# Order of the attention steps, the pool of the transposes and the first products of a fused attention and mixture kernel

## The chip, the core and the metric

The kernel runs on one core of a Trainium2 chip. Time is the device time of one execution in microseconds (us). TensorE multiplies, VectorE and ScalarE take results out of PSUM and work on SBUF, GpSimd works on SBUF alone, and SP issues nearly all transfers.

## What is computed

Three layers, one behind the other. Inputs are drawn at random.

```python
def _attn_ref(q, k, v):                       # 4 batches, 8 heads, 576 positions, 64 features
    scores = scale * np.matmul(q, k.transpose(0, 1, 3, 2))
    mask_local = (rel >= 0) & (rel < stride)  # stride = 32, heads 0 to 3
    mask_strided = (rel >= 0) & (pos[None, :] % stride == pos[:, None] % stride)   # heads 4 to 7
    ...                                       # softmax over the masked scores
    return np.matmul(attn, v)

def _moe_ref(x, w_gate, w1, w2):              # 2304 tokens of 512, 8 experts of 1024
    ...                                       # P: 8 rounds of row and column normalization of the gate
    for e in range(E):
        out += P[:, e:e + 1] * (np.maximum(x @ w1[e], 0.0) @ w2[e])

def _moe2_ref(x, w_in, w_out):                # 512 to 2048 to 512
    h = x @ w_in
    return np.where(h > 0.0, h, np.exp(np.minimum(h, 0.0)) - 1.0) @ w_out
```

## The kernel before, in words

Attention is done in 32 steps `u`, two for each of 16 pairs of heads; two local steps (u % 4 is 0 or 1) alternate with two strided ones (2 or 3). A step has three stages. `att_s2(u)` makes scores: a mask product with the full array (line 529), then products of q and k of 64 features in quarters of the array (line 543). VectorE takes the maximum and subtracts it (552, 553), ScalarE exponentiates (556), VectorE sums (559) and takes reciprocals (564), GpSimd multiplies by them (567, "normalization"). `att_s3` transposes the result on TensorE (605 for local steps, full array; 590 for strided ones, half of the columns), ScalarE copies it out. `att_s4` multiplies by v (628 local, half of the columns; 644 strided, quarters). In step u these run for u, u - 2 and u - 3. What follows the scores is not issued at once: `defer` puts it off by a number of ticks, one tick at each yield of the attention generator, by the tables `DEF_FIRST`, `DEF_ALONE` and `DEF_MIXED`.

The program is written out by Python generators, and the order in which they are advanced is the order of each engine's instructions; no scheduler changes it. Up to step 20 ("mix") attention runs alone, with some products of the mixture put in between: from step 12 on, one "group" of six products of 512 columns behind each step. From step 20 on a piece of attention (four advances of its generator) runs every few `gap`s between products. A gap comes about every three products and also advances the weights' splitting (`prep_step`), the splitting of x (`build_step`) and the gate.

All products of the mixture are made in three matmuls of a high and a low part (xh, xl, w1h, w1l). The first two pairs of 128 features of expert 0 use the features as they are ("direct", lines 1080 to 1105); later ones use sums of quarters (`gemm1`, `gemm2` is the second layer, line 1247). The sums are built from `build_sums` on VectorE (line 379), cast to xh on ScalarE (385) and to xl on VectorE and GpSimd (217). Before the second layer of the first pair all builds that are left are issued at once (`ready("sums")`).

PSUM has two pools of four banks: `bank()` (ps) for scores and first-layer products, `ybank()` (py) for the second layer. `spare_bank()` gives a bank of the first pool while the second layer runs and one of the second otherwise. `warm_up` puts a matmul without use (line 452) into a new bank to keep TensorE busy, until the first "group".

## Time and profile before

| | |
|---|---|
| median of 3 runs | 1992.93 us (1991.99 to 1992.95) |
| the profiled execution | 1992.91 us, of which the span of the core 1991.0 us |
| TensorE busy in the span | 1972.8 us (99%), 10563 matmuls |
| VectorE, ScalarE, GpSimd busy | 1240.1 us, 683.7 us, 601.0 us |
| attention | about the first 165 us |

A busy TensorE is not one at its peak: matmuls overlap, so what counts is the distance from start to start, and idle time where it waits. A row of the timeline gives start, length, engine, line of the kernel, what is written and read, how many instructions are merged, and in brackets how long the engine was idle before and what ended it.

### The profile page before, as it was taken

Reading aid. Unit: us, or ns where it says so; the run is one execution under the profiler, and the core shown is the slowest. Engines: PE = TensorE matmul, PEld = TensorE weight load, DVE = VectorE, ACT = ScalarE, POOL = GpSimd, SP = SyncE. Lnnn points to the kernel's source line nnn. Section 1 sums busy time; section 2 is a strip of 40 time slices with the busy share of each in tenths; the row PEclk is TensorE's granted clock in tenths of the full one; section 3 lists DMA queues with packets and bytes.
Section 4 is the critical chain, followed back from the end, with each engine's and each line's share of the span. In section 5 each row is a group of like instructions: output and inputs, shape, how many; then the busy total and the mean of one; then the engine's idle time right before and its main releaser. Section 6 shows DMA issues by size and latency. Waiting matters only on the chain.

```text
span 1991.0 us, 27182 instructions
## 1 busy us (share of the span) xinstructions
PE 1972.8 (99%) x10563; PEld 1633.1 (82%) x10563; DVE 1240.1 (62%) x2078; ACT 683.7 (34%) x1414; POOL 601.0 (30%) x690
## 2 busy tenths in 40 slices
PE   9999999999999999999999999999999999999999
PEld 7777888888888888888888888888888888887887
DVE  6657666555455657566666666666664485568665
ACT  5543332233223334222222222222222264446543
POOL 4533332333333332222232222222222212233340
PEclk9999999999999999999999999999999999999999
DMA  7422211111113112122222222222221111212111
GB/s 219 146 84 66 64 50 47 53 53 54 53 42 106 54 53 85 64 75 90 75 69 85 80 85 71 83 80 85 65 69 43 43 32 33 85 43 96 43 54 53
DMA packets 82786, 140.79 MB, mean 71 GB/s; under 512 B 5760, under 2 KB 39808, under 8 KB 82656
## 3 DMA queue, kind: packets, MB, share of 16 engines
q1 hardware_dynamic: 81696, 138.83, 22.2%
q8 instruction: 83, 1.36, 0.3%
q14 instruction: 47, 0.39, 0.1%
q10 hardware_dynamic: 960, 0.21, 0.1%
HBM read 121.20 MB, written 17.83 MB: 70 GB/s over the span
## 4 chain that ended last, share of the span: by engine, by line
PE 91%; DVE 4%; ACT 3%; issue 1%; DMA 0%; POOL 0%; DVEq 0%; ACTq 0%; POOLq 0%
PE ybank L1247 48%; PE bank L1017 40%; ACT g L1040 1%; ACT g L1039 1%; DVE u L1131 1%; PE bank L543 1%; ACT hh L1044 1%; DVE xl L217 0%; DVE c L1131 0%; PE ybank L628 0%; PE ybank L605 0%; DVE hl L1034 0%; PE ybank L590 0%; ACT w1h L207 0%; DMA k_t<-in_k 0%
## 5 line engine op out<-in xcount | busy, mean ns | idle before, releaser
L1247 PE MATMUL ybank<-w2h,hh 128*128 128x512 f32 x1280 | 501.8, 392 | 0.3
L1247 PE MATMUL ybank<-w2h,hl 128*128 128x512 f32 x1280 | 499.0, 390 | 0.0
L1247 PE MATMUL ybank<-w2l,hh 128*128 128x512 f32 x1280 | 498.7, 390 | 0.0
L1017 PE MATMUL bank<-xh,w1h 128*128 128x512 f32 x1124 | 443.0, 394 | 3.8 <-DVE u L1131 3.7
L1017 PE MATMUL bank<-xl,w1h 128*128 128x512 f32 x1124 | 438.1, 390 | 0.0
L1017 PE MATMUL bank<-xh,w1l 128*128 128x512 f32 x1124 | 437.9, 390 | 0.0
L217 POOL TENSOR_TENSOR w1l<-w1raw,w1h 128x256 fp32r<-128x256 f32 x244 | 211.1, 886 | 425.4 <-ACT w1h L207 425.2
L1278 DVE SCALAR_TENSOR_TENSOR acc<-ybank,prob,acc 128x512 f32<-128x512 f32 x244 | 182.8, 749 | 229.1 <-PE ybank L1247 228.5
L217 POOL TENSOR_TENSOR w2l<-w2raw,w2h 128x512 fp32r<-128x512 f32 x80 | 103.9, 1298 | 600.0 <-ACT w2h L207 579.5
L1247 PEld LDWEIGHTS ybank<-w2h,hh 128*128 128x128 f32 x1280 | 240.8, 188 | 51.8 <-DVE acc L1264 1.6
L1247 PEld LDWEIGHTS ybank<-w2h,hl 128*128 128x128 f32 x1280 | 240.6, 188 | 50.6
L1247 PEld LDWEIGHTS ybank<-w2l,hh 128*128 128x128 f32 x1280 | 240.8, 188 | 49.0
L207 ACT CAST w2h<-w2raw 128x512 fp32r<-128x512 f32 x160 | 97.1, 620 | 463.4 <-issue 406.7
L1017 PEld LDWEIGHTS bank<-xh,w1h 128*128 128x128 f32 x1124 | 211.1, 188 | 53.3 <-DVE u L1131 8.0
L1017 PEld LDWEIGHTS bank<-xh,w1l 128*128 128x128 f32 x1124 | 211.0, 188 | 44.9
L1017 PEld LDWEIGHTS bank<-xl,w1h 128*128 128x128 f32 x1124 | 211.3, 188 | 40.3
L1131 DVE TENSOR_TENSOR u<-bank,a 128x512 f32<-128x512 f32 x152 | 105.0, 691 | 195.2 <-PE bank L1017 163.4
L236 POOL TENSOR_TENSOR wsum<-w1raw 128x256 f32<-128x256 f32 x152 | 117.5, 773 | 227.7 <-DMA w1raw<-in_moe_w 159.4
L1032 ACT ACTIVATE hh<-bank 128x512 fp32r<-128x512 f32 x193 | 114.8, 595 | 117.6 <-DVE bank L1131 110.7
L1034 DVE SCALAR_TENSOR_TENSOR hl<-bank,hh 128x512 fp32r<-128x512 f32 x193 | 131.8, 683 | 7.1 <-ACT hh L1032 0.9
L217 DVE TENSOR_TENSOR w1l<-wsum,w1h 128x512 fp32r<-128x512 f32 x152 | 112.4, 747 | 10.0 <-ACT w1h L207 8.9
L1032 ACT ACTIVATE hh<-c 128x512 fp32r<-128x512 f32 x61 | 38.6, 633 | 224.4 <-DVE c L1131 224.4
(229 smaller groups left out, 2401.5 us busy)
## 6 DMA issues: line engine op xcount, KB each, us to landing
w1raw<-in_moe_w SPq DMA_DIRECT2D x64, 512.0 KB
w2raw<-in_moe_w SPq DMA_DIRECT2D x64, 512.0 KB
raw<-in_moe_w_in SPq DMA_DIRECT2D x16, 512.0 KB
w_conv<-val SPq DMA_DIRECT2D x32, 256.0 KB
raw<-in_moe_w_out SPq DMA_DIRECT2D x16, 512.0 KB
w1raw<-w_conv SPq DMA_DIRECT2D x16, 512.0 KB
w2raw<-w_conv SPq DMA_DIRECT2D x16, 512.0 KB
q_t<-in_q SPq DMA_DIRECT2D x16, 288.0 KB
```

The lines of the kernel that those rows point to most:

```text
L207: se.copy(hi, src)
L217: eng.tensor_tensor(out=lo, in0=src, in1=hi.bitcast(F32), op=ALU.subtract)
L236: po_.tensor_tensor(out=o, in0=x, in1=y, op=op)
L543: pe.matmul(pp[part][r : r + w, i * nk : (i + 1) * nk], t["q"][dd, qc : qc + w], t["k"][dd, kc : kc + nk], start=False, stop=i == len(mine ...
L1017: pe.matmul(dst, a_[:, wi, c, :], b_[:, xi, c, :], start=start and i == 0, stop=stop and i == 5, skip_group_check=True,)
L1032: se.activation(hh, src, AF.Relu)
L1034: ve.scalar_tensor_tensor(out=hl, in0=src, scalar=0.0, in1=hh.bitcast(F32), op0=ALU.max, op1=ALU.subtract)
L1039: se.activation(g, src, AF.Relu, scale=-1.0)
L1040: se.activation(g, g, AF.Exp, scale=-1.0)
L1131: ve.tensor_tensor(out=out, in0=x, in1=y, op=ALU.add)
L1247: pe.matmul(y, x[:, cs], w[:, f], start=first and f + m == 0, stop=last and f == 1 and m == 2)
L1278: ve.scalar_tensor_tensor(out=at, in0=y, scalar=prob[:, g, e : e + 1], in1=at, op0=ALU.mult, op1=ALU.add)
```

## The change

In the attention part: in steps above 3 with u % 4 of 2 or 3 the transposition comes first, then scores, then values; in the other steps scores, values, transposition. This holds alone and mixed (mixed had values, transposition, scores). The transposition always takes a bank of the second pool. The first products come in a new generator, `first_parts`: each part does one chunk of 128 features for both quarters, and leaves its bank open until the other chunk's part. Ten of the 16 parts run in steps 9, 10 and 12 to 19 (before: eight, in steps 12 to 19). After the second layer starts, attention waits for `HOLD` = 4 gaps. q and k of the second pair are loaded ahead of v of the first. Five constants differ.

```diff
-            pt = warm_up(ybank() if alone_now[0] else spare_bank())
+            pt = warm_up(ybank())
...
-            for gen in (s2, s4, s3, s3) if alone_now[0] else (s4, s3, s3, s2):
+            for gen in (s3, s3, s2, s4) if u > 3 and u % 4 > 1 else (s2, s4, s3, s3):
...
-            if MOE_FROM <= u < MIX_FROM:
+            if u in GROUP_AT:
                 yield "group"
...
+    load_qk(1)
     load_v(0)
-    load_qk(1)
...
+            while second[0] and count[0] < second[1] + HOLD:
+                yield True
...
+    def first_parts():
+        order = [(0, 0, f, c) for c in (0, 1) for f in (0, 1)] + [(1, 0, f, c) for f in (0, 1) for c in (0, 1)]
+        order += [(0, 1, f, c) for c in (0, 1) for f in (0, 1)] + [(1, 1, f, c) for f in (0, 1) for c in (0, 1)]
+        open_ = {}
+        for p, half, f, c in order:
+            prep_state["now"] = p
+            w = slot_of(p, "done1")
+            m = open_.setdefault((p, half, f), None) if c else open_.setdefault((p, half, f), bank())
+            keys = ("B12", B22) if half else (B11, B21)
+            for i, (wi, key) in enumerate(zip((S1, A22) if f else (A11, A12), keys)):
+                need(key, c)
+                for a_, b_ in ((0, 0), (0, 1), (1, 0)):
+                    pe.matmul(m, w[a_][:, wi, c, :], xb[b_][:, T1 if key == "B12" else key, c, :], ...)
...
-        second[0] = True
+        second[:] = [True, count[0]]
...
-WARM0, WARM1, WARM_MOD, WARM_OF, WARM_N = 14, 10, 4, 1, 512
+WARM0, WARM1, WARM_MOD, WARM_OF, WARM_N = 12, 10, 4, 1, 512
-W1_AT, W2_AT = 3, 9
+W1_AT, W2_AT = 2, 9
-DEF_ALONE, DEF_MIXED = (2, 4, 5, 6), (2, 3, 4, 5)
-PREP_AT = 24
-MOE_FROM, MIX_FROM, ATT_RATE = 12, 20, 0.8
+DEF_ALONE = DEF_MIXED = 2, 4, 5, 6
+PREP_AT = 20
+MIX_FROM, ATT_RATE = 20, 0.8
+GROUP_AT = (9, 10, 12, 13, 14, 15, 16, 17, 18, 19)
+HOLD = 4
```

What stands on the engines, at three places. First TensorE in step 18 (attention alone), before, from the last product of step 17's group to the first of step 18's: masks and scores (529, 543), values (644), transposition (605).

```order
L1017 MATMUL bank<-xh,w1l_84 128x512
L529 LDWEIGHTS eye
L529 MATMUL bank<-m_str,eye 118x162
L529 LDWEIGHTS eye
L529 MATMUL bank<-m_str,eye 118x162
L543 MATMUL bank<-k_t,q_t 54x54 x12
L644 MATMUL ybank<-eT,v_t 64x54 x10
L605 MATMUL ybank<-ident,e_local_113 96x128 x5
L1017 MATMUL bank<-xh,w1h_83 128x512
```

The same stretch after.

```order
L1094 MATMUL bank<-xh,w1l_84 128x512
L605 MATMUL ybank<-ident,e_local_113 96x128 x5
L529 LDWEIGHTS eye
L529 MATMUL bank<-m_str,eye 118x162
L529 LDWEIGHTS eye
L529 MATMUL bank<-m_str,eye 118x162
L543 MATMUL bank<-k_t,q_t 54x54 x12
L644 MATMUL ybank<-eT,v_t 64x54 x10
L1094 MATMUL bank<-xh,w1h_81 128x512
```

The transposition moved from the end of the step to its head, right behind the group of the step before. Second, TensorE in step 23 (mixed), before: values (628), transposition, masks and scores, then the second layer.

```order
L628 MATMUL bank<-eT,v_t 64x64 x10
L605 MATMUL bank<-ident,e_local_114 96x128 x4
L529 LDWEIGHTS eye
L529 MATMUL bank<-m_str,eye 118x162
L529 LDWEIGHTS eye
L529 MATMUL bank<-m_str,eye 118x108
L543 MATMUL bank<-k_t,q_t 54x54 x10
```

And after.

```order
L605 MATMUL ybank<-ident,e_local_114 96x128 x4
L529 LDWEIGHTS eye
L529 MATMUL bank<-m_str,eye 118x162
L529 LDWEIGHTS eye
L529 MATMUL bank<-m_str,eye 118x108
L543 MATMUL bank<-k_t,q_t 54x54 x10
L628 MATMUL bank<-eT,v_t 64x64 x10
```

The values moved behind the scores, and the transposition writes to the second pool. Third, VectorE around the reciprocal of step 20 (`rc`, sums `sm` of e_local_113), before.

```order
L553 TENSOR_TENSOR e_local_114<-ybank,ng 128x2x96
L564 RECIPROCAL rc<-sm 128x5
L379 TENSOR_TENSOR acc<-acc 128x512
L1034 SCALAR_TENSOR_TENSOR hl<-bank,hh 128x512
L217 TENSOR_TENSOR w1l_82<-wsum,w1h_81 128x512
L559 TENSOR_REDUCE sm<-e_local_114 128x4
L217 TENSOR_TENSOR xl<-acc,xh 128x512 x2
```

And after.

```order
L553 TENSOR_TENSOR e_local_114<-ybank,ng 128x2x96
L559 TENSOR_REDUCE sm<-e_local_113 128x5
L379 TENSOR_TENSOR acc<-acc 128x512
L217 TENSOR_TENSOR xl<-acc,xh 128x512 x2
L1036 SCALAR_TENSOR_TENSOR hl<-bank,hh 128x512
L217 TENSOR_TENSOR w1l_82<-wsum,w1h_81 128x512
L564 RECIPROCAL rc<-sm 128x5
```

Step 20's reciprocal now stands behind the last builds of the sums; its sum, too, is behind step 21's subtraction.

## Rows read from the trace of the kernel before

**Rows 1.** The page: shares of the chain that ended last; one group's mean.

```profile
PE 91%; DVE 4%; ACT 3%; issue 1%; DMA 0%; POOL 0%; DVEq 0%; ACTq 0%; POOLq 0%
...
L1034 DVE SCALAR_TENSOR_TENSOR hl<-bank,hh 128x512 fp32r<-128x512 f32 x193 | 131.8, 683 | 7.1 <-ACT hh L1032 0.9
```

**Rows 2.** Stretches: length; PE, PEld, DVE, ACT, POOL busy (count); clock; DMA.

```profile
80.00:90.00 10.00, 8.23 (x101) 5.69 (x98) 9.93 (x19) 6.26 (x15) 5.77 (x4) 0.99 0.51 156
90.00:100.00 10.00, 9.80 (x81) 7.26 (x79) 4.30 (x14) 5.76 (x13) 4.17 (x4) 0.84 0.29 84
...
400.00:500.00 100.00, 100.00 (x443) 82.67 (x442) 55.73 (x84) 33.51 (x68) 34.04 (x42) 1.00 0.17 53
```

**Rows 3.** Timeline of TensorE at the start: start, length, instruction [idle before, releaser].

```profile
10.40 0.52 PE L543 MATMUL bank<-k_t,q_t 64*54 64x54 f32 x24 [1.18 <-DMA k_t<-in_k]
...
13.31 0.84 PE L605 MATMUL ybank<-ident,e_local 128*96 128x128 f32 x3
```

**Rows 4.** Timeline of GpSimd at the start: the first normalization.

```profile
11.18 0.99 POOL L567 TENSOR_TENSOR e_local<-e_local,rc 128x480 f32<-128x480 f32 x1 [1.01 <-DVE rc L564]
```

**Rows 5.** Transfers in the first 45 us.

```profile
DMA packets 5983, 10.34 MB, mean 230 GB/s; under 512 B 1192, under 2 KB 2600, under 8 KB 5976
```

**Rows 6.** Timeline of TensorE, attention alone: steps 6, 10, 14 and 18.

```profile
23.01 0.30 PE L529 MATMUL bank<-m_str,eye 118*118 118x162 bf16 x2
...
24.87 0.75 PE L605 MATMUL ybank<-ident,e_local 128*96 128x128 f32 x5 [0.75 <-POOL e_local L567]
...
33.90 0.50 PE L452 MATMUL ybank<-warm 128*128 128x512 f32 x1
...
46.03 0.30 PE L529 MATMUL bank<-m_str,eye 118*118 118x162 bf16 x2
...
47.29 0.75 PE L605 MATMUL ybank<-ident,e_local 128*96 128x128 f32 x5 [0.17 <-POOL e_local L567]
...
59.65 0.30 PE L529 MATMUL bank<-m_str,eye 118*118 118x162 bf16 x2
```

**Rows 7.** Timeline of GpSimd: normalizations for the transpositions of steps 14 and 18.

```profile
45.98 1.26 POOL L567 TENSOR_TENSOR e_local<-e_local,rc 128x480 f32<-128x480 f32 x1 [2.73 <-DVE rc L564]
...
59.60 0.99 POOL L567 TENSOR_TENSOR e_local<-e_local,rc 128x480 f32<-128x480 f32 x1 [1.71 <-DVE rc L564]
```

**Rows 8.** Timeline of TensorE: scores before values (step 13) and before products (step 21).

```profile
42.95 0.56 PE L543 MATMUL bank<-k_t,q_t 64*64 64x96 f32 x16
43.33 0.52 PE L644 MATMUL ybank<-eT,v_t 54*64 54x54 f32 x24
...
80.39 0.56 PE L543 MATMUL ybank<-k_t,q_t 64*64 64x96 f32 x16
80.88 0.50 PE L1017 MATMUL bank<-xh,w1h 128*128 128x512 f32 x1
```

**Rows 9.** Timeline of TensorE in the mixed part: steps 20, 22 and 27.

```profile
73.04 0.69 PE L628 MATMUL ybank<-eT,v_t 96*64 96x64 f32 x16
...
74.27 0.38 PE L529 MATMUL ybank<-m_local,eye 128*128 128x96 bf16 x3
...
85.31 0.56 PE L644 MATMUL bank<-eT,v_t 54*64 54x54 f32 x20
...
87.52 0.42 PE L605 MATMUL bank<-ident,e_local 128*96 128x128 f32 x2 [1.20 <-ACT xlate L654]
88.52 0.30 PE L529 MATMUL bank<-m_str,eye 118*118 118x162 bf16 x2 [0.58 <-DVE hl L1034]
...
121.53 0.21 PE L529 MATMUL ybank<-m_str,eye 118*118 118x108 bf16 x1 [1.06 <-ACT xlate L636]
```

**Rows 10.** Timeline of VectorE: step 20's reciprocal and xl casts.

```profile
82.90 0.18 DVE L564 RECIPROCAL rc<-sm 128x5 f32<-128x5 f32 x1
...
85.43 2.43 DVE L217 TENSOR_TENSOR xl<-acc,xh 128x512 fp32r<-128x512 f32 x2
...
98.03 0.65 DVE L217 TENSOR_TENSOR xl<-acc,xh 128x512 fp32r<-128x512 f32 x1
```

More of the change, by code (lines that the diff above doesn't have):

```diff
@@ L602, in att_s3 @@
             n = min(3, len(tiles) - i0)
-            pt = warm_up(ybank() if alone_now[0] else spare_bank())
+            pt = warm_up(ybank())
             for i in range(n):
@@ L871, in sparse_attention_moe_kernel @@
     gens = []
-    second, hurry = [False], [0]
+    second, hurry = [False, 0], [0]
     def spare_bank():
@@ L1077, in gemm1_two @@
         return hs
+    def first_parts():
[10 more added lines that the diff above has]
+                for a_, b_ in ((0, 0), (0, 1), (1, 0)):
+                    pe.matmul(
+                        m,
+                        w[a_][:, wi, c, :],
+                        xb[b_][:, T1 if key == "B12" else key, c, :],
+                        start=c + i + a_ + b_ == 0,
+                        stop=c + i == 2 and a_ == 1,
+                        skip_group_check=True,
+                    )
+                if i == 0 and not alone_now[0]:
+                    gap()
+            used(p)
+            if c:
+                acts.append(activate(p, m, HALF, h_first[p][f, half]))
+            advance(acts)
+            if not alone_now[0]:
+                gap()
+            yield
     def direct_parts(sg, p):
@@ L1416, in sparse_attention_moe_kernel @@
     rest = None
-    first = [direct_parts(0, p) for p in range(GROUP)]
-    h_first = [next(x) for x in first]
-    parts = (next(x) for x in first for _ in range(4))
+    h_first = [{(f, half): new_h(p) for half in (0, 1) for f in (0, 1)} for p in range(GROUP)]
+    first = first_parts()
     for x in att_gen:
@@ L1424, in sparse_attention_moe_kernel @@
             warming[0] = False
-            next(parts, None)
+            next(first)
             continue
@@ L1475, in memory @@
         return x
-    for x in first:
-        for _ in x:
-            pass
+    for _ in first:
+        pass
     start_build("T1", build_both(T1, b_raw, (ve, po_)))
```

## The prediction, made before the changed kernel was timed

> **What bounds the kernel now.** I read the chain of work first, then the table by stretches, then TensorE's timeline of the attention part beside those of VectorE, GpSimd and the transfers. The chain is TensorE for 91% [rows 1], and in a late stretch TensorE is busy for all of 100 us with 443 matmuls, one start each 0.226 us [rows 2]. The change leaves the number of product matmuls as it is, and nothing after attention is rewritten, so only the first 165 us can move: what counts is TensorE's waste there. It has four kinds: idle while it waits (1.18 us for k_t at 10.40, 0.75 at 24.87, 0.17 at 47.29, 1.20 at 87.52, 1.06 at 121.53) [rows 3, 6, 9]; warm-up matmuls whose result nobody reads [rows 6]; the gap when the array goes from one tile shape to another [rows 8]; and a stretch at half clock: 0.84 granted in 90 to 100 us, that is the 1.2 GHz level for a third of it [rows 2], right after the worst stall. The profiled execution took 1992.91 us with a span of 1991.0; its 1.9 us outside don't change. It is the median of the runs to 0.02 us, so the sum is made against it.
>
> **The start: -1.4 us.** q and k of the second pair are issued ahead of v of the first. v is 96 x 1216 words, 467 KB; at the mean of 230 GB/s [rows 5] k_t lands some 2 us earlier and the 1.18 us are gone [rows 3]. WARM0 takes two matmuls off the head: 0.45 us by the pitch above. The step that then counts is the first transposition of e_local: it started at 13.31 [rows 3], although its operand was ready at 11.18 + 0.99 = 12.17 [rows 4]. With the head 0.45 earlier the operand is there at 11.7; TensorE, 1.18 earlier at 12.1 if the five fillers run as now. So 12.1 less the 13.31 is -1.2, up to -1.6 if they run faster; I take -1.4. The lower bound is -0.4, if k_t gains nothing. v of the first pair now lands later but is first read after these transpositions, 2 us or more away; without that cover it would cost what k_t gains. The first weights' load (W1_AT) is ahead of one pair's q and k on SP's queue: 512 KB, 2.2 us at that rate, while those are read several steps later; I cost it at nothing, 2.2 us if the cover fails.
>
> **Warm-up: -1.3 us.** The warm-ups stop at the first "group", now at step 9. Three of 17 go. One is 0.50 long [rows 6], of which the next group overlaps a little; between 0.23 (the pitch) and 0.50 I take 0.43, so 3 x 0.43. Two products more lie ahead of the mix and two fewer behind it: moved, not saved.
>
> **The new order while attention is alone: +3.5 us.** In steps 6, 7, 10, 11, 14, 15, 18, 19 the transpositions go ahead of scores and values. Scores and values gave the softmax of two steps before time to end; in every fourth step (6, 14, 18; step 10 has the new product at step 9 ahead of it) that cover is gone. The number of tile shape changes doesn't fall here, since a full-array product or mask stands before and after either way. Step 6: TensorE got to its masks at 23.01; the operand was used at 24.87 [rows 6], after an idle 0.75. Started first, it waits 1.86, so +1.1. Step 14: TensorE was free at 46.03, GpSimd's normalization ended at 45.98 + 1.26 = 47.24 [rows 6, 7]: 1.21 + 0.05 less the 0.17 now, +1.1. Step 18: free at 59.65, ready at 59.60 + 0.99 = 60.59 [rows 6, 7]: +0.95. Together +3.1. Behind each wait stand scores and values in TensorE's queue, and VectorE waits for the scores, so nothing fills it. Four smaller places have no row: step 12's scores need a bank of the first pool, of which two are now held open from step 9 to 13; product 14 needs weights that GpSimd makes behind a normalization; steps 8 and 9 transpose strided heads later. Bounds 0 and 1.5; I take 0.4, near the 0.17 that such waits cost now.
>
> **The order in the mixed part: -2.0 us.** Scores followed by values in the same 64x64 shape take 43.33 - 42.95 = 0.38; the same scores followed by a full product take 80.88 - 80.39 = 0.49 [rows 8]: a change of shape costs 0.11 us. Four successive steps have 17 changes now (4, 5, 4, 4) and 11 after (3, 3, 2, 3). Three such rounds have scores: 3 x 6 x 0.11 = 2.0. Bounds 1.3 (two thirds of them seen) and 2.5.
>
> **Transposes in the second pool, HOLD: -0.2 us in sum.** Scores no longer queue behind a copy for a bank: the 1.06 at 121.53 [rows 9] should fall to about 0.4, since the values, now last, still want a bank that ScalarE frees: -0.7, bounds -1.1 and +0.4. New waits of transpositions that go first in steps 22 to 31 have no row; one such wait costs 0.17 to 1.86 in the alone part, but here 15 matmuls (3.4 us) lie between scores and transposition. Bounds 0 and 2.5, I take 0.5.
>
> **Step 20, the costliest place: 0.** In before the burst began at 85.31 and TensorE stood idle for 1.20 and 0.58 in it [rows 9]: 1.8 of waste. The cause is the builds of the sums, all issued at once before the second part's products. After, the reciprocal of step 20 stands behind them: one more subtraction, two xl casts, one hl and one w1l are ahead of it. The casts took 2.43 [rows 10], the other three about 0.68 each by hl's mean [rows 1]: 4.5. Its scores start 74.27 - 73.04 = 1.2 us earlier, as values and transposition no longer stand ahead of them [rows 9], so the reciprocal goes from 82.90 [rows 10] to 82.9 + 4.5 - 1.2 = 86.2, and with a normalization as long as the 1.26 of step 14 [rows 7] the operand is there at 87.4. TensorE comes at 85.0 (85.31 less three changes of shape in the two bursts before): 2.4 of waste instead of 1.8. If the casts run at the 0.65 of a lone one [rows 10], it is 1.3 (1.13 less). I take no change, bounds -1.0 and +1.5. HOLD's delay doesn't shorten this: 30 matmuls lie between the scores and the transposition before and after. The half-clock stretch behind it I leave: 0, bound -1.7 (a third of 10 us at half speed).
>
> **The sum.** -1.4 - 1.3 + 3.1 + 0.4 - 2.0 - 0.7 + 0.5 + 0 = -1.4: 1992.9 - 1.4 = **1991.5 us**. A measurement of this kernel can tell some 0.2%, 4 us: below 1988.9 is faster, above 1996.9 slower.
>
> **Rivals.**
> (a) The stall at step 20 closes and the clock stays up: -1.8 there instead of 0, -1.7 for the clock. With 1991.5 that gives 1988.0, faster. For it: the low clock follows the stall, and ScalarE, which also made TensorE wait there [rows 9], is freed by the later transposition. Against: VectorE is busy 9.93 of 10 us in 80 to 90 [rows 2], and the reciprocal goes to the end of that queue. Chance 0.26.
> (b) The transposition at the head waits in the mixed part too. In the alone part the operand comes 1.2 us after TensorE is free for it (47.24 against 46.03), behind what VectorE has to do for the next step's scores; in the mixed part VectorE also has the combinations of products in that queue. It decides once that queue takes longer than the 15 matmuls (3.4 us) and the values that lie between. Steps 22, 23, 26, 27, 30, 31 at 1.0 to 1.2 each (the price of step 14) instead of 0.5 in sum: +6.2, so 1997.7, slower. Against: among TensorE's waits after 75 us none is for a normalization, though there too VectorE had both. Chance 0.14.
> (c) The order saves no drain, because a shape change hides under weight loads or waits that come anyway: the -2.0 is not there, 1993.5, within 0.2%. Against: the two intervals of 0.38 and 0.49. Chance 0.15.
> (d) The waits of the alone part don't come, since VectorE reaches the sums earlier there: -3.1, 1988.4, just faster. Chance 0.06; the ends of the normalizations in rows 7 speak against it.
> (e) The two moved casts bring their whole contended length into the path of step 20: 2.4 instead of 1.8, +0.6, so 1992.1, within 0.2%. Two took 2.43 while GpSimd made the same casts for the other half; a lone one took 0.65 [rows 10]. Chance 0.05. The Trainium skill, "SBUF — State Buffer", section "SBUF: two separate sides", says that GpSimd and a VectorE instruction with two SBUF inputs take turns on a port pair, each locking it for a whole instruction; the trace agrees in that the casts are longer in that company, and by that rule this is the case that comes.
>
> **How the numbers follow.** The forecast as worked out has 0.34. Its own bounds run from 1989.9 (start -1.6, step 20 -0.5, none of the smaller and the mixed waits) to 1996.2 (start -0.4, smaller waits 1.5, mixed waits 2.5, step 20 +0.6), so it lies within 0.2%. Same: 0.34 + 0.15 + 0.05 = 0.54. Faster: 0.26 + 0.06 = 0.32. Slower: 0.14. The range goes 1 us below rival (a) and stops short of (b), 1986.9 to 1996.9: below it lies a small part of (a), above it most of (b), less than 0.2 together.
>
> **What would show it.** After the change: no idle for k_t, the first transposition of e_local near 12; three fewer warm-ups; idle ended by GpSimd before transpositions at steps 6, 14, 18, of 1 to 2 us each, which are my largest cost; bursts of the mixed part shorter by 0.1 to 0.3 us each; one idle piece at step 20 of 1 to 3 us, ended by GpSimd where ScalarE ended it, and a stretch at half clock after it. I am wrong if those waits of the alone part are missing, if the clock is 1.00 from 80 to 110 us, or if anything after attention differs by more than 1 us.

## The result and the profile after

The changed kernel takes 2002.65 us (2002.28 to 2003.48), against 1992.46 us for the kernel before in the same comparison: 1.0052 times as long, interval 1.0040 to 1.0065. That is 11 us above the forecast and 6 us above its range. With every term at its worst bound (covered loads left out) the prediction's sum would have ended near 1999.5, so the miss is not one of sizes alone.

The span of the profiled execution is 2001.7 us, against 1991.0. To see where the 10.7 us lie I cut both traces at two instructions that both programs have: the second block of gate products (L661, 67.36 us in before, 76.95 after), which comes right after the mix begins, and the first product behind attention (L916, now L918; 169.91 and 188.58). Columns: stretch; its length; busy time of PE, PEld, DVE, ACT, POOL (count); granted clock; DMA. The first stretch begins with the first mask of step 0. Before:

```profile
6.25:67.36 61.11, 58.65 (x1035) 45.32 (x1034) 42.79 (x129) 37.81 (x96) 30.36 (x45) 0.97 0.78 229
67.36:169.91 102.55, 98.10 (x1063) 72.97 (x1063) 62.99 (x150) 45.64 (x107) 38.95 (x44) 0.98 0.27 86
```

After:

```profile
6.44:76.95 70.51, 61.84 (x1044) 47.05 (x1043) 43.18 (x128) 37.16 (x95) 31.20 (x46) 0.98 0.66 194
76.95:188.58 111.63, 103.97 (x1093) 79.99 (x1093) 67.97 (x155) 48.54 (x112) 37.91 (x44) 0.97 0.26 79
```

Alone, the part is 9.4 longer; 12 products that were moved into it take 2.7 (0.226 each), which leaves **+6.7**. TensorE is not busy for 8.7 us there, against 2.5. Mixed, the part is 9.1 longer; 30 more matmuls (1093 against 1063) are 6.8 of that, which leaves **+2.3**. The rest of the program has 42 products fewer (9.5 us) and is only 8.0 shorter: **+1.5**, in code that the change doesn't touch. Busy times of VectorE, ScalarE and GpSimd in the first part hardly differ: no engine has more to do, TensorE waits more often. These are the waits (timeline of TensorE, attention alone; steps 6, 8, 12, 14, 16 and 18), which answer to [rows 6]:

```profile
23.39 0.75 PE L605 MATMUL ybank<-ident,e_local 128*96 128x128 f32 x5 [1.67 <-POOL e_local L567]
30.36 0.83 PE L590 MATMUL ybank<-ident,e_str 118*64 118x118 f32 x12 [1.22 <-POOL e_str L567]
...
41.99 0.30 PE L529 MATMUL bank<-m_local,eye 128*128 128x96 bf16 x2 [1.50 <-DVE e_str L553]
42.47 0.24 PE L529 MATMUL bank<-m_local,eye 128*128 128x192 bf16 x1 [0.18 <-DVE e_str L553]
...
53.64 0.75 PE L605 MATMUL ybank<-ident,e_local 128*96 128x128 f32 x5 [1.56 <-POOL e_local L567]
62.42 0.83 PE L590 MATMUL ybank<-ident,e_str 118*64 118x118 f32 x12 [0.47 <-POOL e_str L567]
...
69.03 0.75 PE L605 MATMUL ybank<-ident,e_local 128*96 128x128 f32 x5 [0.84 <-POOL e_local L567]
```

And in the mixed part (steps 21, 22, 25, 29 and 31; what step 22 transposes is step 20's), which answer to [rows 9]:

```profile
90.07 0.83 PE L590 MATMUL ybank<-ident,e_str 118*64 118x118 f32 x12 [0.61 <-ACT xlate L654]
...
97.86 1.30 PE L605 MATMUL ybank<-ident,e_local 128*96 128x128 f32 x5 [2.53 <-POOL e_local L567]
...
119.64 0.83 PE L590 MATMUL ybank<-ident,e_str 118*64 118x118 f32 x12 [0.66 <-DVE e_local L553]
...
147.80 0.82 PE L590 MATMUL ybank<-ident,e_str 118*64 118x118 f32 x12 [0.66 <-DVE e_local L553]
...
161.07 0.80 PE L628 MATMUL ybank<-eT,v_t 96*64 96x64 f32 x20 [1.68 <-issue]
```

After three of the longest waits, and after one of 1.85 us at 1844, TensorE ran at the 1.2 GHz level for a while (table of stretches of the changed kernel; the last column but two is the granted clock):

```profile
40.00:50.00 10.00, 8.32 (x155) 6.50 (x151) 5.43 (x16) 5.15 (x13) 2.62 (x3) 0.83 0.45 133
...
100.00:110.00 10.00, 10.00 (x105) 8.32 (x101) 4.24 (x13) 5.74 (x14) 5.66 (x7) 0.94 0.44 136
160.00:170.00 10.00, 8.93 (x58) 6.54 (x60) 7.40 (x18) 2.59 (x7) 1.02 (x1) 0.83 0.17 54
1840.00:1850.00 10.00, 8.15 (x30) 6.21 (x29) 7.62 (x11) 6.76 (x13) 5.46 (x5) 0.83 0.17 54
```

The kernel before had two such stretches, near 11 and 90 us. What one costs can be read off directly: two executions of the same program up to 66 us, one with such a stretch in the alone part (the row 6.25:67.36 above, clock 0.97) and one without (the kernel called before_phase_other below):

```profile
6.17:65.64 59.47, 57.24 (x1035) 44.17 (x1035) 42.77 (x129) 37.75 (x96) 30.33 (x45) 1.00 0.77 233
65.64:166.58 100.94, 96.49 (x1063) 71.80 (x1063) 63.01 (x150) 45.57 (x107) 38.87 (x44) 1.00 0.28 88
```

61.11 - 59.47 = **1.64 us** for one stretch; the mixed parts of the two, with the same idle time, give 1.61. In what follows lengths are compared at full clock, with 1.64 taken off for each such stretch (some later traces have a stretch of twice the length; the clock column then shows 0.95 over the alone part instead of 0.97 or 0.98): 59.5 for the alone part of the kernel before, 100.9 for its mixed part. The medians of many executions hold the average of the stretches that come and go.

### The profile page after: what moved, and what is told of

Read it like the earlier page. It is cut to its first block, busy times and chain, and to the rows that moved or that the text cites. A ratio compares the mean times of both kernels' runs of the same rounds, so it can differ in the third digit from the quotient of the medians.

```text
span 2001.7 us, 27163 instructions
## 1 busy us (share of the span) xinstructions
PE 1974.5 (99%) x10558; PEld 1635.1 (82%) x10558; DVE 1241.8 (62%) x2078; ACT 683.7 (34%) x1414; POOL 597.9 (30%) x690
## 4 chain that ended last, share of the span: by engine, by line
PE 92%; DVE 4%; ACT 3%; issue 1%; POOL 1%; POOLq 0%; ACTq 0%; DVEq 0%
PE ybank L1280 48%; PE bank L1019 39%; PE bank L1094 1%; ACT g L1042 1%; ACT g L1041 1%; DVE u L1164 1%; PE ybank L590 1%; ACT hh L1046 0%; PE bank L543 0%; PE ybank L605 0%; DVE xl L217 0%; POOL e_local L567 0%; DVE c L1164 0%; DVE g L1044 0%; PE ybank L628 0%
## 5 line engine op out<-in xcount | busy, mean ns | idle before, releaser
L1019 PE MATMUL bank<-xh,w1h 128*128 128x512 f32 x1092 | 430.7, 394 | 4.1 <-DVE u L1164 3.9
L1019 PE MATMUL bank<-xl,w1h 128*128 128x512 f32 x1092 | 426.8, 391 | 0.0
L1019 PE MATMUL bank<-xh,w1l 128*128 128x512 f32 x1092 | 426.4, 391 | 0.0
L1019 PEld LDWEIGHTS bank<-xh,w1h 128*128 128x128 f32 x1092 | 205.6, 188 | 53.3 <-DVE u L1164 7.9
L1019 PEld LDWEIGHTS bank<-xh,w1l 128*128 128x128 f32 x1092 | 205.6, 188 | 43.9
L1019 PEld LDWEIGHTS bank<-xl,w1h 128*128 128x128 f32 x1092 | 205.8, 189 | 39.7
```

The costliest lines, as they stand in the source:

```text
L1019: pe.matmul(dst, a_[:, wi, c, :], b_[:, xi, c, :], start=start and i == 0, stop=stop and i == 5, skip_group_check=True,)
```

## The experiments

In each, "before" is the time of the kernel before on the same chip in the same comparison.

**The counter at the hand-over.** The plus 1.5 far from the change needs a cause. The generator that mixes the work counts gaps, and in the second half of the mixture builds of sums are skipped at every third count. Since two first products moved ahead of the mix, where no gap is counted for them, the count is 4 lower from there to the end, and 4 is not a multiple of 3. Two kernels shift that line alone.

```diff
-        if not part2 or count[0] % 3:
+        if not part2 or (count[0] + 1) % 3:
```

> The changed kernel, with the counter of gaps advanced by one in the single line that skips every third build of sums in the second half of the mixture: (count + 1) % 3. Nothing before the last quarter of the program reads this line. Theory P (phase): two of the first products moved ahead of the mix, the counter is 4 lower from there on, 4 is not a multiple of 3, so builds and casts at the hand-over to the third layer come in another order; there TensorE waits 0.56 and 1.85 us (before: 1.64 alone) and a stretch at half clock follows. Advanced by one, the order is that of the kernel before: some 3 us come back, 1999.7, no half clock after 1800 us. Rival D (drift): the hand-over is late because everything is some 8 us later against the transfers; then nothing comes back, 2002.6.

```diff
-        if not part2 or count[0] % 3:
+        if not part2 or (count[0] + 2) % 3:
```

> The kernel before, with (count + 2) % 3 in the same line, which is the phase that the changed kernel has there. Theory P: it loses what the changed kernel loses at the hand-over: 1992.5 + 2.9 = 1995.4, with waits of about 0.6 and 1.8 us near 1830 and a half-clock stretch behind them. Rival D: 1992.5.

after_phase: 2001.30 us (1999.39 to 2002.16), where the changed kernel had 2002.65 and, on another chip, 2003.78. before_phase: 1993.70 (before 1992.84; ratio 1.0004, interval 0.9994 to 1.0014). The medians alone wouldn't decide, the rows do. Timeline of TensorE at the hand-over from the second to the third layer, in the changed kernel:

```profile
1834.83 0.47 PE L1019 MATMUL bank<-xh,w1h 128*128 128x512 f32 x1 [0.56 <-DVE u L1164]
1844.14 0.50 PE L1019 MATMUL bank<-xh,w1h 128*128 128x512 f32 x1 [1.85 <-DVE u L1164]
```

after_phase has one wait there:

```profile
1841.63 0.50 PE L1019 MATMUL bank<-xh,w1h 128*128 128x512 f32 x1 [1.64 <-DVE u L1164]
```

In the kernel before:

```profile
1835.07 0.50 PE L1017 MATMUL bank<-xh,w1h 128*128 128x512 f32 x1 [1.64 <-DVE u L1131]
```

And in before_phase:

```profile
1826.20 0.47 PE L1017 MATMUL bank<-xh,w1h 128*128 128x512 f32 x1 [0.56 <-DVE u L1131]
1835.51 0.50 PE L1017 MATMUL bank<-xh,w1h 128*128 128x512 f32 x1 [1.87 <-DVE u L1131]
```

The pattern goes with the phase, in both kernels and both ways: theory P holds, drift falls. Counted from the end of the program, matmuls 700 to 500 take 47.3 us in before and after_phase, 48.7 in before_phase, and 50.3 in the changed kernel, where the clock fell behind the second wait. So the phase costs 1.5 us, and 3.0 in executions where the clock falls; it fell in three of the seven traces with this pattern. In before_phase's trace it didn't, and its median lies 1.7 below the 1995.4 of theory P.

The third phase:

```diff
-        if not part2 or count[0] % 3:
+        if not part2 or (count[0] + 1) % 3:
```

> The kernel before with (count + 1) % 3 in the line that skips every third build late in the program: the phase that neither kernel has. Theory P: the wait at the hand-over to the third layer depends on this phase; in the other two it is 1.64, or 0.56 and 1.87. This one lies at 0.8 to 2.5 us in sum, 1991.5 to 1993.2, and nothing before 1600 us changes. Rival D: 1.64, as before.

1992.18 us (before 1992.29; 0.9999, 0.9990 to 1.0008), with the single wait of 1.64 again. Of three phases one loses, and the change fell on that one. This trace has no stretch at half clock before its last microsecond (span 1988.1 us), and so it is the measure for the others.

**The order while attention is alone.**

```diff
-            for gen in (s3, s3, s2, s4) if u > 3 and u % 4 > 1 else (s2, s4, s3, s3):
+            for gen in (s3, s3, s2, s4) if u > 3 and u % 4 > 1 and not alone_now[0] else (s2, s4, s3, s3):
```

> The changed kernel with the order of before (scores, values, transposition) in the steps in which attention is alone; mixed steps keep the new order. Theory H (head): the waits for GpSimd at the head of steps 6, 8, 10, 14, 16, 18 (1.67, 1.22, 0.19, 1.56, 0.47, 0.84) fall to those of before (0.75, 0.18, 0.17): -4.9, 1997.8. If the wait of 1.68 at step 12 and the half clock behind it also come from that order, -8, 1994.6. Rival M (moved): VectorE is the bound of this part, the waits come back at other places, 2001 to 2003.

1997.65 us (before 1992.84; ratio 1.0022, 1.0012 to 1.0031), 5.0 below the changed kernel's first median, as theory H has it. The head waits went, and the step-12 wait with them. Two others appeared, in the products:

```profile
48.76 0.75 PE L605 MATMUL ybank<-ident,e_local 128*96 128x128 f32 x5 [0.63 <-POOL e_local L567]
52.05 0.79 PE L1094 MATMUL bank<-xh,w1l 128*128 128x512 f32 x1 [1.97 <-POOL w1l L217]
74.29 0.50 PE L1094 MATMUL bank<-xl,w1h 128*128 128x512 f32 x1 [0.74 <-POOL xl L217]
```

The first products now reach weights, and once a part of x, before GpSimd has split them; the new order had hidden this by being late itself. Idle in the alone part fell by 3.1 (8.7 to 5.6), so rival M, by which all of it only moves, falls, though 2.7 us did move to these two places. The ten runs lie apart: three took 1993.0 to 1994.3 us at a mean granted clock of 0.999 to 1.000, seven 1997.0 to 1999.6 at 0.996 to 0.997, so the 5.0 between the medians hold the clock too. The same question from the other side, the new order in the kernel before, in the alone steps and nowhere else:

```diff
-            for gen in (s2, s4, s3, s3) if alone_now[0] else (s4, s3, s3, s2):
+            for gen in ((s3, s3, s2, s4) if u > 3 and u % 4 > 1 else (s2, s4, s3, s3)) if alone_now[0] else (s4, s3, s3, s2):
```

> The kernel before with the new order (transposition, scores, values) in steps 6, 7, 10, 11, 14, 15, 18, 19 alone; all else as before, and no bank is held open. Theory H: the order alone brings the head waits of the changed kernel, 1.67, 1.22, 1.56, 0.47, 0.84 at steps 6, 8, 14, 16, 18 in place of 0.75, 0.18, 0.17: +4.7, and it makes the subtraction of step 11 so late that step 12 waits 1 us or more though no bank is held: +5.7, 1998.2. Theory B (banks held open are half of it): no wait at step 12, the wait at step 8 not there either since the heads behind it differ: +3.1 as the prediction had it, 1995.5.

1999.42 us (before 1992.29; ratio 1.0043, 1.0027 to 1.0060; four runs of 1997.8 to 2004.0): **+7.1 us** from this line alone. Its stretches, alone and mixed:

```profile
6.88:73.88 67.00, 59.36 (x1035) 45.29 (x1034) 43.00 (x128) 37.29 (x95) 30.75 (x46) 0.97 0.70 204
73.88:174.84 100.96, 96.51 (x1064) 71.81 (x1063) 63.25 (x150) 45.90 (x108) 37.81 (x43) 1.00 0.27 88
```

The mixed part is that of before to 0.02 us; the alone part is 67.0 - 1.64 - 59.5 = 5.9 longer at full clock, and 5.4 of that is idle (7.6 against 2.2). The waits up to step 14:

```profile
23.82 0.75 PE L605 MATMUL ybank<-ident,e_local 128*96 128x128 f32 x5 [1.68 <-POOL e_local L567]
29.82 0.83 PE L590 MATMUL ybank<-ident,e_str 118*64 118x118 f32 x12 [0.24 <-POOL e_str L567]
34.93 0.75 PE L605 MATMUL ybank<-ident,e_local 128*96 128x128 f32 x5 [1.76 <-POOL e_local L567]
42.87 0.83 PE L590 MATMUL ybank<-ident,e_str 118*64 118x118 f32 x12 [0.44 <-POOL e_str L567]
50.75 0.75 PE L605 MATMUL ybank<-ident,e_local 128*96 128x128 f32 x5 [1.10 <-POOL e_local L567]
```

Steps 16 and 18 wait 0.47 and 0.84, as in the changed kernel. Step 10 waits 1.76 here, where no product stands at step 9; with that product, in the changed kernel, it waits 0.19. Step 12's scores don't wait here, where no bank is held, and step 8 waits 0.24 instead of 1.22. In size theory H is right, in its account of steps 8 and 12 theory B. So I took the held bank away in the changed kernel.

```diff
-        order = [(0, 0, f, c) for c in (0, 1) for f in (0, 1)] + ...
+        order = [(0, 0, f, c) for f in (0, 1) for c in (0, 1)] + ...
```

> The changed kernel with the first four parts in the order quarter by quarter instead of chunk by chunk, so that one bank of the first pool is held open and only from one part to the next (steps 9 to 10), none at step 12. Theory B (banks): the 1.50 and 0.18 at step 12 are scores without a bank; they go, and the stretch at half clock behind them with them: -1.7 - 1.7, 1999.3. Rival L (late): the subtraction of step 11 is late because of the waits at the heads; the wait stays whatever is held, 2002.6. The weights of the second chunk are needed one part earlier, which may cost up to 1 us at step 10.

2001.90 us (before 1992.84; 1.0046, 1.0031 to 1.0061): nothing gained that can be told from the changed kernel's 1.0052. The wait at step 12 is gone, so the bank was what the scores waited for; but TensorE's busy time in the alone part (62.02 of 70.72) says that just as much is lost elsewhere:

```profile
40.37 0.50 PE L1094 MATMUL bank<-xh,w1h 128*128 128x512 f32 x1 [1.11 <-ACT xh L207]
...
46.62 0.83 PE L590 MATMUL ybank<-ident,e_str 118*64 118x118 f32 x12 [0.80 <-POOL e_str L567]
```

Banks explain where the wait stood, not that there is one: neither theory as put.

**The first products.** What they cost when everything else is put back (old orders, old pool and mixed table, `HOLD` 0, phase of before):

```diff
-            for gen in (s3, s3, s2, s4) if u > 3 and u % 4 > 1 else (s2, s4, s3, s3):
+            for gen in (s2, s4, s3, s3) if alone_now[0] else (s4, s3, s3, s2):
...
-            pt = warm_up(ybank())
+            pt = warm_up(ybank() if alone_now[0] else spare_bank())
...
-        if not part2 or count[0] % 3:
+        if not part2 or (count[0] + 1) % 3:
...
-DEF_ALONE = DEF_MIXED = 2, 4, 5, 6
+DEF_ALONE, DEF_MIXED = (2, 4, 5, 6), (2, 3, 4, 5)
-HOLD = 4
+HOLD = 0
```

> The changed kernel with everything put back but the first products and the start: old order alone and mixed, transposes in the pool of before, HOLD = 0, old table for the mixed part, the phase of the counter as before. What is left: products by chunk from step 9 on in ten parts, the load order, 12 warm-ups at the head and the two start counts of the splitting. Theory W (weights): three warm-ups fewer give -1.3, but products come before GpSimd has split their weights: waits of about 2.0 at step 15 and 0.7 at step 19, seen with the old order alone; +1.4, and step 20 as before: 1993.7. Rival: those waits come from the mixed table or the pool; then -1.3, 1991.0.

1995.81 us (before 1992.29; 1.0018, 1.0008 to 1.0028): +3.5, with the waits of 1.97 and 0.75 as expected. That is 2.1 more than theory W had. Its trace has stretches at half clock (0.95 over the alone part, 0.97 over the mixed one), a wait of 1.49 at 128.95 where before has 1.06, and one for step 20's operand, though the mixed order is the old one:

```profile
95.00 1.20 PE L605 MATMUL bank<-ident,e_local 128*96 128x128 f32 x5 [2.17 <-POOL e_local L567]
```

Here the reciprocal had ended at 90.64; the normalization stood behind a cast of xl on GpSimd itself (91.94 to 93.54). Now the same with eight parts from step 12 on, without the shift of the phase:

```diff
-GROUP_AT = (9, 10, 12, 13, 14, 15, 16, 17, 18, 19)
+GROUP_AT = (12, 13, 14, 15, 16, 17, 18, 19)
```

> As the kernel with only the new first products left (old orders, old pool, old mixed table, HOLD = 0), but they begin at step 12 in eight parts; with eight parts ahead of the mix the counter is that of the kernel before, so no phase is set. Theory W (too early): the waits of 1.97 and 0.75 for weights and sums at steps 15 and 19 were those of two parts more ahead of the mix; they go, the three warm-ups come back (+1.3): 1992 to 1992.6. Rival C (chunk): the second pair's weights are needed in its first part whatever the start, since a chunk is taken for both quarters of features; waits of 1 us or more remain: 1993.5 to 1994.5.

1993.57 us (before 1992.07; 1.0007, 0.9998 to 1.0017). Both waits are gone and the alone part is 59.65 us at full clock, 0.2 from before. The time would suit rival C; but what is lost stands in the mixed part (103.24 - 1.64 = 101.6 against 100.9), and not in waits for weights. Theory W holds: the early start made the waits, not the chunks.

**The mixed part.**

```diff
-            for gen in (s3, s3, s2, s4) if u > 3 and u % 4 > 1 else (s2, s4, s3, s3):
+            for gen in (s4, s3, s3, s2) if not alone_now[0] else (s3, s3, s2, s4) if u > 3 and u % 4 > 1 else (s2, s4, s3, s3):
```

> The changed kernel with the old order (values, transposition, scores) in the mixed steps; alone it keeps the new one. Theory F (five banks): a mixed step puts its scores, values and transposition into up to five banks of the second pool, which has four, so what comes last waits for VectorE or ScalarE to free one; before, the last was the scores, after, the transposition at steps 21, 25, 29 (0.61, 0.66, 0.66) or the values at 159 us (1.68, with a half-clock stretch of 1.7 behind it). With the old order these go (-4.6), the 1.06 of before at step 27 comes back (+0.8), the changes of shape cost 1.2 more, and step 20 waits 2.0 instead of 2.5: 2002.65 - 3.1 = 1999.5. Rival Q (VectorE's queue): the waits are for VectorE, whatever the order; they stay in sum, and the 1.2 is lost: 2003.9.

2002.70 us (before 1992.23; 1.0054, 1.0039 to 1.0069). The waits at steps 21, 25, 29 and 31 went, as theory F says, and idle in the mixed part fell from 7.7 to 5.6; but two of 0.62 and 1.02 came, step 20 waits 2.77 where F had 2.0, and the time is the same. F names the waits rightly and overrates what they bring. The other side, the new order in the mixed part of the kernel before:

```diff
-            for gen in (s2, s4, s3, s3) if alone_now[0] else (s4, s3, s3, s2):
+            for gen in (s2, s4, s3, s3) if alone_now[0] else (s3, s3, s2, s4) if u % 4 > 1 else (s2, s4, s3, s3):
```

> The kernel before with the new order in the mixed steps alone; pools, HOLD, the first products and the alone part stay as before. Theory F: -1.2 for the changes of shape, -0.8 at step 27, +2.0 for the transpositions at 21, 25, 29, +1.7 and up to +1.7 of clock for the values near step 31, +0.5 at step 20: 1992.5 + 3 = 1995.5. The forecast of the prediction for this part alone: -2.0, 1990.5.

1993.69 us (before 1992.23; 1.0007, 0.9997 to 1.0016), between theory F's 1995.5 and the forecast's 1990.5. No stretch at half clock in this trace, so it compares directly with 100.94 and its 4.4 of idle:

```profile
66.34:168.21 101.87, 94.09 (x1064) 72.26 (x1064) 62.62 (x150) 46.25 (x107) 38.40 (x44) 1.00 0.26 87
```

The time from a matmul to the next at a change of operation (idle taken off), summed over the 101 changes of this stretch, falls from 19.6 to 18.2 us: the order does save 1.4. Another 1.0 is saved between matmuls inside the transpositions and masks; idle rises by 3.3, so the part gets 0.9 longer. Beside 1.60 at 86.90, where before has 1.20 and 0.58, the waits are new ones, these among them:

```profile
105.78 0.83 PE L590 MATMUL bank<-ident,e_str 118*64 118x118 f32 x12 [0.66 <-DVE e_local L553]
...
118.91 0.80 PE L628 MATMUL ybank<-eT,v_t 96*64 96x64 f32 x20 [1.26 <-issue]
```

The first waits until VectorE has left the scores of its own step; both writers share a pool of four banks. What ended the second ("issue") the profile doesn't name; VectorE's first subtraction of that step's scores ended 0.10 us ahead of it, at 118.81, and in the changed kernel at 160.98, 0.09 ahead of 161.07, which fits a bank but doesn't show it. What remained was whether pool and table, which the change alters together with the order, matter.

```diff
-            pt = warm_up(ybank() if alone_now[0] else spare_bank())
+            pt = warm_up(ybank())
...
-            for gen in (s2, s4, s3, s3) if alone_now[0] else (s4, s3, s3, s2):
+            for gen in (s2, s4, s3, s3) if alone_now[0] else (s3, s3, s2, s4) if u % 4 > 1 else (s2, s4, s3, s3):
...
-DEF_ALONE, DEF_MIXED = (2, 4, 5, 6), (2, 3, 4, 5)
+DEF_ALONE = DEF_MIXED = 2, 4, 5, 6
```

> The kernel before with the new order in the mixed part, the transposes in the second pool and the new table of deferrals; alone, first products and HOLD as before. Theory S (set): order, pool and table belong together; the mixed part, 100.9 us at full clock in the kernel before and 101.9 with the order alone, is 100.1 as in the changed kernel with HOLD = 0: 1991.5, with fewer waits at steps 22 and 26 than with the order alone (3.3 more than before). Rival O (order): five banks are wanted whatever the pool; 101.9, 1993.5.

**1988.46 us** (1987.69 to 1989.52; before 1992.07; ratio 0.9983, interval 0.9973 to 0.9993): faster than both kernels. Its mixed part, by the table of stretches:

```profile
66.08:164.85 98.77, 93.72 (x1063) 72.02 (x1063) 65.00 (x150) 46.35 (x107) 37.75 (x44) 1.00 0.29 89
```

Its longest waits there, from TensorE's timeline:

```profile
79.65 0.83 PE L590 MATMUL ybank<-ident,e_str 118*64 118x118 f32 x12 [1.10 <-DVE e_local L553]
87.12 0.46 PE L644 MATMUL bank<-eT,v_t 54*64 54x54 f32 x16 [0.98 <-DVE hl L1034]
...
117.58 0.80 PE L628 MATMUL ybank<-eT,v_t 96*64 96x64 f32 x20 [1.26 <-issue]
```

98.8 against 100.9 at full clock, -2.2: idle is 5.0 instead of 7.8 with the order alone. The rest of the 3.6 goes with the clock: all ten runs have a mean granted clock of 1.000, of the 19 runs of before in that comparison only two, and these two took 1990.00 and 1990.11, so at that clock 1.6 us are left between the kernels. This trace has no stretch at half clock in the part and no wait over 1.3.

**The hold, and the start.**

```diff
-HOLD = 4
+HOLD = 0
```

> The changed kernel with HOLD = 0: attention goes on as soon as the second layer starts. Theory S (queue of sums): at step 20 GpSimd's normalization comes so late because the reciprocal stands behind the builds of the sums on VectorE; both sides move together, so the wait stays at 2.5, and the bank waits stay: 2002 to 2003.5. Rival T (time given): the four gaps of three matmuls (2.7 us) are what keeps the wait this short; without them it is up to 5.2: 2005.3.

2001.13 us (before 1992.23; 1.0046, 1.0031 to 1.0061); step 20 waits 2.55, as with `HOLD` = 4. Theory S holds, rival T falls: the hold does nothing for step 20. But it costs something. The mixed part without it:

```profile
76.54:179.96 103.42, 96.79 (x1063) 74.44 (x1063) 63.99 (x151) 46.52 (x108) 36.05 (x42) 0.97 0.28 86
```

With the hold it is 111.63 at the same clock, less 6.8 for 30 more matmuls 104.9: **1.4 us** longer, 1.0 of it idle (7.7 against 6.6). Three other traces with the hold, this order and this clock (after_again, after_phase, after_old_alone) have 111.4 to 111.7; without it there is this one.

```diff
-    load_v(0)
     load_qk(1)
+    load_v(0)
...
-WARM0, WARM1, WARM_MOD, WARM_OF, WARM_N = 14, 10, 4, 1, 512
+WARM0, WARM1, WARM_MOD, WARM_OF, WARM_N = 12, 10, 4, 1, 512
```

> The kernel before with q and k of the second pair loaded ahead of v of the first, and 12 warm-ups at the head. Prediction's term: -1.4, 1991.1. In the changed kernel step 4 began 1.48 earlier, but a wait of 0.98 for GpSimd took the place of the 1.18 for k_t, and what came back is that the five fillers ran at full clock. Theory K (clock): so this gives -0.3 to -0.5 where the clock falls at the start in both, and -1.5 to -2 where it falls in before alone; near 1991.5. If the load order alone makes the difference, -1.4 in every run.

1992.08 us (before 1992.23; 0.9999, 0.9990 to 1.0008). The load order gives nothing; as theory K says, the wait for k_t is gone and one of 0.96 for GpSimd stands in its place.

**The changed kernel again.** The same program on the chip of before_new_alone, after_parts and before_phase_other.

> The changed kernel as it is, on the chip of the three others, to have all sizes from one chip and a second profile of the same program. 2002.65 by the first measurement. Theory K (clock): the stretches at half clock lie at other places than 43.26, 97.87, 162.72 and 1845.49, though each still follows a wait, and single runs differ by 1.7 per stretch; waits of TensorE are the same to 0.05 us. Rival: the stretches belong to the program and return at the same places.

2003.78 us (before 1992.29; 1.0058, 1.0043 to 1.0073). At the hand-over the clock fell behind the same wait as in the first profile. In the mixed part it fell at step 20's wait alone, for twice as long, and not behind the 1.68 near 163; in the alone part it fell at 20 to 30 us, not at 43, and for twice as long (clock 0.95 over the part, against 0.98). One wait changed by more than was expected (step 8: 0.27). Between theory K and its rival: a stretch follows some wait, but which one differs.

## Why the prediction was wrong, step by step

The step that failed most is in the alone part: places without a row, taken at 0.4, cost 3.4. Beside it stand terms that were put at nothing and measured more: the clock, the code behind attention, the hold, and step 20.

**The start, -1.4: wrong.** In the profile of before, the first transposition of e_local came 13.31 - 6.25 = 7.06 us after the first mask; in before_phase and before_phase_other, the same program up to there, it came 5.98 after it. Most of the 1.08 between them is TensorE at half clock (0.83 granted in 10 to 20 us): from step 2's late scores, at 10.40, to that transposition it took 2.91, in before_phase 2.26 for the same instructions. The other 0.4 is k_t, which came 0.4 later in that execution. Before that k_t was hardly a bound: in before_phase_other it came in time, and the same place waited for the softmax instead:

```profile
12.15 0.53 PE L605 MATMUL ybank<-ident,e_local 128*96 128x128 f32 x3 [0.96 <-POOL e_local L567]
```

I had the sign of it in [rows 4]: a normalization that ends at 12.17. The step that failed is "the 1.18 us are gone": the clock aside, all but 0.4 of them were slack, since the softmax ended only 5.9 us after the first mask with or without them (12.17 - 6.25 in before, 12.10 - 6.17 in before_phase_other).

**Warm-ups, -1.3.** Three fewer are there; what they bring was not measured by itself. The products that end them cost 3.5 in after_parts, clock and step 20's wait included, in part by waits that the prediction had among the smaller places ("product 14 needs weights that GpSimd makes behind a normalization").

**The order while alone, +3.5: right in cause, too small.** The three places with a row came out as priced in sum: steps 6, 14 and 18 cost 0.92, 1.39 and 0.84 more than before, 3.15 against 3.1. The step that failed is "four smaller places have no row ... I take 0.4": steps 8, 10, 12 and 16 cost 1.22 + 0.19 + 1.68 + 0.47, less the 0.18 of step 9 before: 3.4, over its bound of 1.5; step 16 was not on the list at all. I had priced each place as if the rest kept its time. But a wait at the head stands before that step's scores, so its softmax starts later, and the next transposition that goes without cover waits again. The rows fit that (before_new_alone has waits at every even step from 6 to 18); no run changes one head alone. GpSimd's timeline of the changed kernel, ahead of the transpositions of steps 14 and 18:

```profile
52.34 1.24 POOL L567 TENSOR_TENSOR e_local<-e_local,rc 128x480 f32<-128x480 f32 x1 [4.03 <-DVE rc L564]
...
67.98 0.99 POOL L567 TENSOR_TENSOR e_local<-e_local,rc 128x480 f32<-128x480 f32 x1 [2.94 <-DVE rc L564]
```

It stood idle 4.0 and 2.9 us ahead of operands that TensorE waited for, longer than the 2.7 and 1.7 before [rows 7]. TensorE is busy for 88% of this part and VectorE for 61%, so no engine is the bound; what is left, by argument, is the time of one step's chain from scores to transposition, and the cover of it was what the change gave away.

**The mixed part, -2.0 - 0.2.** The order saves 1.4 of shape changes, near the lower bound of 1.3. The set of order, pool and table together gives the forecast's -2.2, but by luck in part: 1.6 from changes of operation (19.6 to 17.9) and 1.1 inside transpositions and masks, less 0.6 of more idle. In the changed kernel it isn't there: idle is 7.7 where the set has 5.0. The hold, which had no price of its own in the prediction, makes 1.0 of that, and the waits at steps 21 to 23 make 0.7 (3.14 against the set's 1.10 + 0.98 + 0.37). At step 20 the prediction had the queue right: the reciprocal stands behind the last subtraction, two xl casts, hl and w1l, 4.6 us (91.61 to 96.22) where I had 4.5. VectorE's timeline of the changed kernel:

```profile
91.61 0.68 DVE L379 TENSOR_TENSOR acc<-acc 128x512 f32<-128x512 f32 x1
92.21 2.39 DVE L217 TENSOR_TENSOR xl<-acc,xh 128x512 fp32r<-128x512 f32 x2
94.52 0.68 DVE L1036 SCALAR_TENSOR_TENSOR hl<-bank,hh 128x512 fp32r<-128x512 f32 x1
95.12 1.18 DVE L217 TENSOR_TENSOR w1l<-wsum,w1h 128x512 fp32r<-128x512 f32 x1
96.22 0.18 DVE L564 RECIPROCAL rc<-sm 128x5 f32<-128x5 f32 x1
```

GpSimd's, right behind it:

```profile
96.47 1.34 POOL L567 TENSOR_TENSOR e_local<-e_local,rc 128x480 f32<-128x480 f32 x1 [0.73 <-DVE rc L564]
```

I had worked out 2.4 of wait and then took "no change", the middle between 2.4 and 1.3; it was 2.53, and 0.61 at step 21 (1.98 in before, with the 0.20 behind it: +1.2, inside the bounds). The casts had their contended length, 2.39, while GpSimd made two of the other half (92.56 to 95.75), so rival (e) describes this place, as the rule cited there from the Trainium skill ("SBUF — State Buffer", section "SBUF: two separate sides") would have it. In before_mixed_set the reciprocal is ahead of hl, w1l and xl, and step 20's transposition doesn't wait; there the count is 4 higher when the second layer starts, since no first products were moved ahead of the mix.

**Nothing after attention: wrong.** "Nothing after attention is rewritten, so only the first 165 us can move" overlooked that the order there is made by a counter that the change shifts. Of the 10.7 us, 3.0 arose at the hand-over (half of it a stretch at half clock, counted below too), and 1.2 of it was won back where two short waits behind attention shrank (0.74 at 193.02 went, 0.72 near 245 became 0.22).

**The clock, left at 0: wrong.** The changed kernel's profile has four stretches, before has two: +3.3 us. I had treated the stretch at 90 us as part of its place; it is there in some executions and not in others (of the five traces whose mixed part is that of before, three have it (before, before_phase, before_start) and two don't (before_phase_other, before_new_alone)).

**The rivals.** (b), slower, was to come from normalizations late in the mixed part; of its six places only step 22 waited for one (the 2.53 priced under step 20), most waits there were for banks by theory F, and the largest loss came from the alone part. (a), (c) and (d) didn't happen. The sign of being wrong that the prediction named, more than 1 us behind attention, did come.

Set against one another by single runs: alone order +7.1, first products with the start +3.5, mixed order, pool and table -3.6, phase +0.9 (up to 3 where the clock falls). That makes 7.9 where 10.2 to 11.5 were measured. The hold adds some 1.5, measured in the changed kernel (2001.13 without it against 2002.65). The remaining 1 to 2 us no run divides: the medians hold the clock, which falls at other waits in each kernel, and the terms meet. Step 20's wait for GpSimd, for one, comes with the ten early parts under either mixed order (2.17 in after_parts, 2.77 in after_old_mixed, 2.53 in the changed kernel), so it is in more than one term.

## What to carry to other kernels

Where no engine is the bound, price a reordering by the chain that it uncovers, all along, not place by place: each wait moves the start of the next chain. Where a counter sets the order, take the remainder of every period that reads it before and after the change, to the end of the program; and before a stall is counted as a gain, look whether the operand behind it was ready any earlier.

## What the runs showed of the chip

A fall of TensorE's clock to the 1.2 GHz level costs this kernel 1.64 us (61.11 against 59.47 us for the same 1035 matmuls). In these traces it comes during or right behind waits of 1.18 to 2.77 us, but not with each of them: of four traces with a wait of 1.87 us at the hand-over, after_one_bank's shows it and those of before_phase, after_old_alone and after_old_mixed don't. So executions of one program differ: the kernel before took from 1990.0 to 1994.2 us in one comparison.
